# Two-stage set attention with a mixture of experts on one core: weights into score buffers, an eleventh x tile, and a new order of all steps

## The chip, the cores and the metric

One core of a Trainium2 chip runs the whole kernel. Its engines are PE (matrix products), DVE (vector), ACT (scalar), POOL (GpSimd) and SP, which issues the DMAs. The metric is the device time of one execution in microseconds (us), as a median of several runs. The language puts one instruction stream on each engine; waits between engines are semaphores.

## The reference

x has 4 batches (B) of N = 11456 rows of C = 128 floats; `inducing` has m = 32 rows. Everything is float32.

```python
def mab(q, kv):
    a = softmax(scale * (q @ kv.T))      # over kv, scale = 1/sqrt(C)
    return a @ kv
h = mab(I, x)        # per batch: 32 x 128 out of 11456 rows
t = mab(x, h)        # per batch: 11456 x 128
out = t.copy()       # then the mixture of experts on all B*N rows of t
do = t @ w_skip > 0
e = argmax(t[do] @ w_gate)                       # one of 8 experts
out[do] += prob(e) * (relu(t[do] @ w1[e]) @ w2[e])   # w1 128 x 1024, w2 1024 x 128
```

## The kernel before

A batch is cut into six groups of 1920 columns (the last 1856) of x transposed, [128, columns]; a group is one x tile of 960 KB, loaded by one DMA into one of ten buffers. Fourteen score buffers ("v", 128 x 960), three for transposed x ("xt"), three for exponentials ("e"), and eight PSUM banks ("banks") are shared the same way.

Per batch the program makes these steps. `load`: the x tiles, and for groups 2 and 3 of batches 1 to 3 also strips of x into v. `first` (lines 318 to 453): scores of x against the inducing rows on PE (L336), their maxima on DVE (L340, which also copies them into a v buffer), the common maximum (L345 on DVE, turned by PE at L348, L352 on DVE, spread by PE at L357), exponentials on ACT (L369), their transposition on DVE (L375), x transposed by PE (L379, copied out by ACT or DVE through the helper at L265/L267) or by DVE from strips (L388), and the sum over the tokens on PE (L395). `middle`: the division by the sums (DVE L472, "den"), the expert of the batch (L517 to L522), its weights read by SP (L651, L652) into an xt buffer, the expert applied to the 32 rows (`g_of` L571, `y_of` L624), the rows that turn a token's logits into relative ones (`lrq`, POOL L563). `second` for each unit of two groups (batch 3: two units of two, then two of one group, its half units): scores on PE (L679), transposition and maximum on DVE (L683, L685, one step `tokens`), the subtraction (L688, `less`, on POOL or DVE), exponentials on ACT, `fold` on POOL (L697), the sums (L701), division (L706, `norm`, POOL or DVE), transposition back (L713), gate logits on PE (L758), their transposition and largest (L762, L764, one step `relative_q`), the gate (L782, L783), `to_streams` on PE (L793), `scale2` (L801, a multiply of the whole tile by the gate, on POOL or DVE), and back again (L713). `emit` then makes the sums on PE (L845), copies them out by ACT or DVE, and SP stores them. `marking` and `judge` (L890 to L949) gather whether any token has another expert than its batch; if so a guarded path (`others`) corrects it, which is not entered with this data.

The order of all steps is a string, ORDER, decoded by `in_order` (L71): each entry names a step, one engine out of those that it allows, and the numbers of the buffers that it takes. Every engine runs its steps in that order, so an engine that waits holds back all that stands behind.

Of the kernel before, what the change touches and what calls it, by code (L numbers as in the profile page):

```python
# [9 lines left out]
F32 = mybir.dt.float32  # L10
# [60 lines left out]
def in_order(ops):  # L71
# [44 lines left out]
def kernel(  # L116
# [70 lines left out]
    sel = const.tile([P, 2 * M], F32, name="sel")
    nc.gpsimd.tensor_tensor(out=sel, in0=ident[:, 0:2 * M], in1=ident[:, 2 * M:], op=ALU.add)
    nc.gpsimd.tensor_tensor(out=sel[:, 0:M], in0=sel[:, 0:M], in1=sel[:, M:], op=ALU.add)
    nc.gpsimd.tensor_copy(out=rep.rearrange("p (q m) -> p q m", q=Q), in_=sel[:, 0:M].unsqueeze(1).broadcast_to([P, Q, M]))  # L190
# [8 lines left out]
    rows = const.tile([P, B, 2, M], F32, name="rows")  # L199
# [118 lines left out]
    def first(s, k):  # L318
# [135 lines left out]
    def middle(s):  # L454
# [119 lines left out]
        o, f = mm(g_of, "gr", s.o_hc, o_w)  # L574

# [51 lines left out]
        o, f = mm(y_of, "yp", o_g, o_w)  # L627
        o.free = [bg]
        L.add("POOL", lambda o: mend(o), o, free=[bw])

        def mend(o):
            nc.gpsimd.memset(xts[bw.idx][:, :, P:P + 1], 1.0)
# [15 lines left out]
    def load_w(e, t):  # L648
        t = t.rearrange("p i c -> p (i c)")
        w1s, w2s = t[:, 0:F], t[:, F:2 * F]  # L650
        nc.sync.dma_start(out=w1s, in_=w1[bass.ds(e, 1), :, :].rearrange("o c f -> c (o f)"))  # L651
        nc.sync.dma_start(out=w2s, in_=w2[bass.ds(e, 1)].rearrange("o p k c -> p (o k c)"))  # L652
# [482 lines left out]
```

## Time and profile before

| | before |
|---|---|
| median of 3 runs | 196.78 us (196.52 to 197.05) |
| profiled execution, its own time | 196.1 us |
| its span (first to last instruction) | 194.4 us |
| busy: PE, DVE, ACT, POOL | 172.8, 154.8, 111.2, 116.0 us |
| share of the span: PE, DVE, ACT, POOL | 89%, 80%, 57%, 60% |
| first DMA queue (x, strips, stores, weights) | 57.02 MB, 82.9% of the span |
| mean granted PE clock | 0.962 |

The slices of the page show PE busy at eight tenths or more in most of the span, DVE from about 50 us on, and both falling off at the end. The profiled execution is 0.68 us shorter than the median. The chain of work that ended last is 37% PE, 23% DVE and 22% DMA. No engine is the bound throughout, so below the span is cut where batch 0, 1, 2 and 3 reach L472, and where the last transposition back (L713) and the last sums (L845) end.

### The profile page before, as it was taken

How to read it: one execution, taken by the hardware profiler on the slowest of the kernel's cores; microseconds unless marked ns; L12 is line 12 of the kernel's file. 1: busy time of each engine (PE TensorE's matmuls, PEld its weight loads, DVE VectorE, ACT ScalarE, POOL GpSimd, SP SyncE). 2: the span in 40 equal slices, each digit the busy share in tenths (PEclk: the TensorE clock that was granted, in tenths of full speed). 3: DMA queues.
4: the chain of work that ended last, by engine and by line, in shares of the span. 5: the costliest groups of instructions: out<-in, count | busy, mean ns of one | idle time of the engine just before them, and what ended most of it. 6: DMA issues, size and time to landing. Idle time of an engine off the chain costs nothing.

```text
span 194.4 us, 5859 instructions
## 1 busy us (share of the span) xinstructions
PE 172.8 (89%) x2331; PEld 102.4 (53%) x2332; DVE 154.8 (80%) x288; ACT 111.2 (57%) x171; POOL 116.0 (60%) x225
## 2 busy tenths in 40 slices
PE   7998899997899999999999988999899698977910
PEld 7574684354687544366876523668545223423310
DVE  0455484798999989999999998999799988988320
ACT  3041680046981685887857564997356836597420
POOL 8200000276768669449986968687847987688510
PEclk9999999999999999999999999999999969999665
DMA  6999992789799799899997999489966995868690
GB/s 187 432 426 415 424 292 58 237 297 254 256 407 199 242 335 358 275 352 403 353 364 155 317 342 366 94 253 348 417 240 220 367 403 199 317 249 335 275 355 12
DMA packets 16881, 57.47 MB, mean 296 GB/s; under 512 B 2384, under 2 KB 7504, under 8 KB 16848
## 3 DMA queue, kind: packets, MB, share of 16 engines
q1 hardware_dynamic: 16560, 57.02, 82.9%
q8 instruction: 19, 0.31, 0.6%
q14 instruction: 14, 0.11, 0.2%
q10 hardware_dynamic: 288, 0.02, 0.1%
HBM read 33.58 MB, written 23.46 MB: 293 GB/s over the span
## 4 chain that ended last, share of the span: by engine, by line
PE 37%; DVE 23%; DMA 22%; ACT 5%; SPq 4%; issue 4%; POOL 2%; DVEq 0%; POOLq 0%; ACTq 0%
DMA x<-in_xT_dram 15%; PE banks L845 10%; PE banks L395 8%; PE banks L379 6%; DMA out_dram<-v 5%; DVE ts L685 3%; PE banks L336 3%; DVE e L683 3%; PE banks L679 3%; ACT v L265 3%; DMA v<-in_xT_dram 2%; DVE v L340 2%; PE banks L758 2%; DVE v L713 2%; SPq L279 2%
## 5 line engine op out<-in xcount | busy, mean ns | idle before, releaser
L265 ACT COPY v<-banks 128x960 f32<-128x960 f32 (+2 forms) x48 | 42.1, 935 | 9.3 <-PE banks L845 9.3
L688 POOL TENSOR_TENSOR e<-e,ts 128x960 f32<-128x960 f32 (+1 forms) x12 | 21.0, 1752 | 38.9 <-DVE ts L685 34.3
L265 ACT COPY xt<-banks 128x1024 f32<-128x1024 f32 (+1 forms) x31 | 28.9, 964 | 20.5 <-PE banks L379 20.4
L379 PE MATMUL banks<-ident,x 128*128 128x128 f32 x270 | 33.6, 276 | 0.0
L379 PEld LDWEIGHTS banks<-ident,x 128*128 128x128 f32 x270 | 29.4, 141 | 4.9 <-issue 1.7
L845 PE MATMUL banks<-v,hr 32*128 32x480 f32 (+1 forms) x192 | 28.5, 618 | 1.0 <-ACT v L265 1.0
L713 DVE STREAM_TRANSPOSE v<-e 128x960 f32<-128x960 f32 (+1 forms) x26 | 28.0, 1080 | 0.9 <-POOL e L801 0.2
L845 PE MATMUL banks<-v,yr 32*128 32x480 f32 (+1 forms) x192 | 26.6, 578 | 0.0
L395 PE MATMUL banks<-xt,v 128*32 128x129 f32 x720 | 25.0, 275 | 1.7 <-DVE v L375 1.1
L336 PE MATMUL banks<-x,iT_sb 128*32 128x480 f32 (+4 forms) x232 | 23.9, 503 | 1.6 <-DMA x<-in_xT_dram 1.6
L395 PEld LDWEIGHTS banks<-xt,v 128*32 128x32 f32 x720 | 20.8, 109 | 6.8 <-issue 2.1
L801 POOL TENSOR_TENSOR e<-e,gs 128x960 f32<-128x960 f32 x11 | 20.9, 1898 | 5.4 <-ACT gs L265 5.4
L679 PE MATMUL banks<-x,hc 128*32 128x480 f32 x192 | 22.5, 586 | 0.4 <-ACT hc L265 0.4
L706 POOL TENSOR_TENSOR e<-e,ts 128x960 f32<-128x960 f32 (+1 forms) x11 | 19.2, 1748 | 5.2 <-DVE ts L703 4.0
L340 DVE TENSOR_SCALAR_CACHE_REDUCE v<-banks 128x960 f32<-128x960 f32 (+1 forms) x13 | 13.9, 1067 | 9.1 <-PE banks L336 8.6
L691 ACT ACTIVATE e<-e 128x960 f32<-128x960 f32 (+1 forms) x13 | 12.3, 949 | 13.1 <-POOL e L688 11.0
L845 PEld LDWEIGHTS banks<-v,yr 32*128 32x128 f32 x192 | 11.5, 192 | 9.4 <-issue 8.6
L375 DVE STREAM_TRANSPOSE v<-v 128x960 f32<-128x960 f32 (+1 forms) x13 | 14.0, 1087 | 2.7 <-ACT v L369 2.6
L683 DVE STREAM_TRANSPOSE e<-banks 128x960 f32<-128x960 f32 (+1 forms) x13 | 14.1, 1086 | 1.3 <-PE banks L679 1.2
L845 PEld LDWEIGHTS banks<-v,hr 32*128 32x128 f32 x192 | 9.7, 189 | 9.4 <-issue 4.0
L685 DVE TENSOR_REDUCE ts<-e 128x30 f32<-128x960 f32 (+1 forms) x13 | 14.0, 1076 | 0.4
L369 ACT ACTIVATE v<-v,bias 128x960 f32<-128x960 f32 (+1 forms) x13 | 13.1, 1032 | 0.6 <-DVE bias L267 0.4
(147 smaller groups left out, 235.3 us busy)
## 6 DMA issues: line engine op xcount, KB each, us to landing
out_dram<-v SPq DMA_DIRECT2D x40, 480.0 KB, 4.5
x<-in_xT_dram SPq DMA_DIRECT2D x19, 960.0 KB, 9.6
v<-in_xT_dram SPq DMA_DIRECT2D x48, 120.0 KB, 6.7
xt<-in_w_dram SPq DMA_DIRECT2D x8, 512.0 KB, 5.4
x<-in_xT_dram SPq DMA_DIRECT2D x4, 928.0 KB, 8.1
out_dram<-v SPq DMA_DIRECT2D x6, 464.0 KB, 3.6
out_dram<-v SPq DMA_DIRECT2D x4, 232.0 KB, 2.7
x<-in_xT_dram SPq DMA_DIRECT2D x1, 512.0 KB, 4.0
```

What stands on the lines that cost most here:

```text
L265: nc.scalar.copy(out=out, in_=in_)
L336: nc.tensor.matmul(ps[q * M:(q + 1) * M, t * M:(t + v.shape[1]) * M].rearrange("m (t r) -> m t r", r=M), lhsT=iT_sb, rhs=v, start=True, st ...
L379: nc.tensor.transpose(out=pair(bp.idx)[:, j // Q, j % Q * P:(j % Q + 1) * P], in_=slot(s.xnow[g])[:, c:c + P], identity=ident)
L395: nc.tensor.matmul(ph[i * M:(i + 1) * M, 0:P + 1], lhsT=aT[:, j, t * M:(t + 1) * M], rhs=xts[bx.idx][:, t, :], start=begin and t < Q, stop ...
L679: nc.tensor.matmul(pair(bs.idx)[q * M:(q + 1) * M, j, 0:WB], lhsT=s.hc[:, 0:M], rhs=slot(bx)[:, G.s2[q]:G.s2[q] + WB], start=True, stop=True)
L683: nc.vector.transpose(out=by_j(ev(M)), in_=pair(bs.idx)[:, 0:n, 0:WB].rearrange("p j (t m) -> p j t m", m=M))
L685: nc.vector.tensor_reduce(out=mx[:, 0:nb], in_=ev(M), axis=AX.X, op=ALU.max)
L688: on(o).tensor_tensor(out=ev(M), in0=ev(M), in1=wide(st["mx"]), op=ALU.subtract)
L706: on(o).tensor_tensor(out=ev(M), in0=ev(M), in1=wide(st["i"]), op=ALU.mult)
L713: nc.vector.transpose(out=st[f"u{k}"][:, 0:W].rearrange("p (t m) -> p t m", m=M), in_=ev(M))
L801: on(o).tensor_tensor(out=ev(M), in0=ev(M), in1=wide(st["gm"]), op=ALU.mult)
L845: nc.tensor.matmul(pair(bp[q // 2].idx)[:, q % 2, 0:G.w1], lhsT=m[r, :], rhs=st[k][r, c:c + G.w1], start=(k == "u1"), stop=(k == "u2"))
```

## The change

The weights no longer share the xt buffers: `w1` and `w2` take a v buffer each, by two steps of SP, and POOL no longer restores the ones of an xt buffer (`mend`). With v tiles of 1024, xt tiles of 15 blocks instead of 16, and small tiles of the guarded path moved into the ends of xt tiles, room is made for an eleventh x tile.

```diff
-    BUFS = {"x": 10, "v": 14, "xt": 3, "e": 3, "lt": 3, "gsel": 1, "fd": 2}
+    BUFS = {"x": 11, "v": 14, "xt": 3, "e": 3, "lt": 3, "gsel": 1, "fd": 2}
...
-    shapes = {"x": [GC], "v": [2, WB], "fd": [WIDE * HALF], "lt": [2 * NQ * E]}
+    shapes = {"x": [GC], "v": [VW], "fd": [WIDE * HALF], "lt": [2 * NQ * E]}
...
-    xts = [const.tile([P, 2 * F // P, P + 1], F32, name=f"xt{i}") for i in range(BUFS["xt"])]
+    xts = [const.tile([P, -(-GC // P), P + 1], F32, name=f"xt{i}") for i in range(BUFS["xt"])]
...
-            st["w1"], st["w2"] = load_w(e1, xts[bw.idx])
-
-        bw = Buf("xt")
-        o_w = L.add("SP", weights, o_c, take=[bw])
+            st["e1"], st["w1"] = e1, slots["v"][b1.idx]
+            load_1(e1, st["w1"])
+
+        def weights2(o):
+            st["w2"] = slots["v"][b2.idx]
+            load_2(st["e1"], st["w2"])
+
+        b1, b2 = Buf("v"), Buf("v")
+        o_w = L.add("SP", weights, o_c, take=[b1])
+        o_w2 = L.add("SP", weights2, o_c, behind=[o_w], take=[b2])
```

`tokens` and `relative_q` are cut in two steps each (the same instructions, which ORDER may now put apart). The maxima of the gate logits are no longer kept to the end: `claim_q` subtracts on the spot (one more small POOL instruction a unit), and the four POOL pairs of `theirs` (L919, L920) are gone.

```diff
+        def highest(o):
             mx = st["mx"] = tsmall[be.idx][0]
             nc.vector.tensor_reduce(out=mx[:, 0:nb], in_=ev(M), axis=AX.X, op=ALU.max)
...
+        def largest_q(o):
+            mx = st["gx"] = gsmall[blt.idx][1]
             nc.vector.tensor_reduce(out=mx[:, 0:nq], in_=qv()[:, :, 0:E - 1], axis=AX.X, op=ALU.max)
...
+            nc.gpsimd.tensor_tensor(out=p, in0=p, in1=t, op=ALU.subtract)
...
-        o_n = L.add("POOL", theirs, *s.o_claim)
```

The guarded path loads its weights in eight pieces and x in four, and one more memset stands inside it. ORDER is new from end to end, of which a line shows nothing:

```diff
-    "000006100H11001090J1207200I20K20810092D0O1320Q110R302080A20B140C20U100D150E20F30G2C0M30P30N2B0i1110k120l20307040605050V1"
+    "0000010A061007200H1100I302090J120K308100O1120P30Q120R3092D0A20B100U130308040705060C20D120E30i1010F30G2C0k113005310432033"
```

By it, three of the five copies of transposed x on DVE go to ACT; the one `less` on DVE (a half unit, L688) goes to POOL; of the `scale2` multiplies DVE has two full ones and a half one where it had two half ones. PE's work and the bytes moved are the same in all.

On PE, around the common maximum of batch 1 (a row is line, operation, output<-inputs, shape and count; x tiles and buffers carry the program's numbers). Before:

```order
L336 MATMUL banks<-x_150,iT_sb 32x480 x4
L336 MATMUL banks<-x_149,iT_sb 32x448 x4
L336 MATMUL banks<-x_149,iT_sb 32x32 x4
L379 MATMUL banks<-ident,x_145 128x128 x8
L571 MATMUL banks<-xt_194,hc_517 32x256 x4
L348 MATMUL banks<-ident,low_1_648 1x128
L357 MATMUL banks<-ones,rows 32x1 x4
L584 MATMUL banks<-ident,g_0_646 128x128 x2
L379 MATMUL banks<-ident,x_145 128x128 x7
L758 MATMUL banks<-v_159,lrq_200 32x256 x4
L395 MATMUL banks<-xt_193,v_158 32x129 x15
```

The same place after the change (L348, L360, L369 and L391 there are L336, L348, L357 and L379 of before):

```order
L348 MATMUL banks<-x_143,iT_sb 32x448 x4
L348 MATMUL banks<-x_143,iT_sb 32x32 x4
L703 MATMUL banks<-x_134,hc_514 32x480 x4
L703 MATMUL banks<-x_144,hc_514 32x480 x4
L391 MATMUL banks<-ident,x_139 128x128 x7
L360 MATMUL banks<-ident,low_1_594 1x128
L348 MATMUL banks<-x_142,iT_sb 32x480 x4
L369 MATMUL banks<-ones,rows 32x1 x4
L391 MATMUL banks<-ident,x_138 128x128 x15
L348 MATMUL banks<-x_141,iT_sb 32x480 x4
L784 MATMUL banks<-v_145,lrq_196 32x256 x4
```

Scores of batch 2 (x_142, x_141) now stand between the turn and the spread and behind them, a whole tile's transposition instead of half a one, and the sum over the tokens comes later.

On DVE, in the last stretch, where batch 3's half units begin. Before:

```order
L611 TENSOR_REDUCE gmax<-banks 128x8
L683 STREAM_TRANSPOSE e_133<-banks 128x15x32
L685 TENSOR_REDUCE ts_0_171<-e_133 128x15
L688 TENSOR_TENSOR e_133<-e_133,ts_0_171 128x15x32
L701 TENSOR_REDUCE sums<-e_134 128x15
L703 RECIPROCAL ts_1_174<-sums 128x15
L713 STREAM_TRANSPOSE v_160<-e_135 128x960
```

After (L707, L711 and L830 are L683, L685 and L801 of before):

```order
L707 STREAM_TRANSPOSE e_127<-banks 128x15x32
L788 STREAM_TRANSPOSE lt_161<-banks 128x256
L711 TENSOR_REDUCE ts_2_168<-e_127 128x15
L830 TENSOR_TENSOR e_125<-e_125,gs_2_184 128x30x32
L792 TENSOR_REDUCE gs_0_171<-lt_161 128x32
L739 STREAM_TRANSPOSE v_153<-e_125 128x960
...
L830 TENSOR_TENSOR e_126<-e_126,gs_0_174 128x30x32
L792 TENSOR_REDUCE gs_2_181<-lt_163 128x16
L739 STREAM_TRANSPOSE v_150<-e_126 128x960
```

The half subtraction left DVE, and two whole multiplies by the gate came to it.

On PE, at the end. Before:

```order
L845 MATMUL banks<-v_165,hr_1915 128x480 x4
L845 MATMUL banks<-v_160,yr_2181 128x480 x4
L845 MATMUL banks<-v_153,hr_1915 128x464 x4
L845 MATMUL banks<-v_163,yr_2181 128x464 x4
L893 MATMUL banks<-ident,lo_2296 1x128
```

After (L876 and L924 are L845 and L893 of before):

```order
L876 MATMUL banks<-v_154,hr_1849 128x464 x4
L876 MATMUL banks<-v_156,yr_2187 128x464 x4
L876 MATMUL banks<-v_152,hr_1849 128x480 x4
L876 MATMUL banks<-v_145,yr_2187 128x480 x4
L924 MATMUL banks<-ident,lo_2360 1x128
```

The last group and the one before it changed places.

## Rows read from the trace of the kernel before

**Rows 1.** Busy time by stretch: length, then each engine's busy us, clock, DMA share, GB/s

```profile
core 0: us, PE busy (x) PEld busy (x) DVE busy (x) ACT busy (x) POOL busy (x), PEclk, DMA share, GB/s
0.00:31.84 31.84, 28.95 (x388) 21.94 (x393) 14.43 (x28) 11.64 (x16) 5.54 (x46) 1.00 0.91 341
31.84:62.40 30.56, 28.14 (x422) 17.20 (x422) 27.98 (x49) 15.18 (x23) 17.82 (x26) 1.00 0.82 256
62.40:100.85 38.45, 38.45 (x556) 22.76 (x555) 36.85 (x63) 28.13 (x41) 28.43 (x42) 1.00 0.95 338
100.85:138.81 37.96, 35.95 (x548) 21.95 (x550) 35.16 (x69) 25.61 (x38) 29.40 (x40) 1.00 0.87 277
138.81:181.10 42.29, 37.02 (x405) 16.45 (x405) 38.33 (x73) 27.34 (x47) 32.55 (x63) 0.94 0.78 301
181.10:184.30 3.20, 3.20 (x25) 1.29 (x17) 0.29 (x1) 1.82 (x2) 1.39 (x7) 0.71 0.51 202
184.30:194.40 10.10, 1.09 (x5) 0.80 (x4) 1.71 (x9) 1.53 (x4) 0.83 (x4) 0.60 0.50 191
```

**Rows 2.** DVE's instructions by line and shape: count, busy us, mean ns, idle before

```profile
L713 DVE STREAM_TRANSPOSE v<-e 128x960 f32<-128x960 f32 x22 | 25.4, 1155 | 0.8 <-POOL e L801 0.2 <-issue 0.2
L340 DVE TENSOR_SCALAR_CACHE_REDUCE v<-banks 128x960 f32<-128x960 f32 x11 | 12.6, 1142 | 3.0 <-PE banks L336 2.5 <-DMA out_dram<-v 0.5
L701 DVE TENSOR_REDUCE sums<-fd 128x30 f32<-128x510 f32 x9 | 5.9, 653 | 0.0
L762 DVE STREAM_TRANSPOSE lt<-banks 128x256 f32<-128x256 f32 x11 | 4.6, 422 | 1.1 <-PE banks L758 1.1
L764 DVE TENSOR_REDUCE gxs<-lt 128x32 f32<-128x224 f32 x11 | 4.2, 386 | 0.4
L701 DVE TENSOR_REDUCE sums<-e 128x30 f32<-128x990 f32 x2 | 2.3, 1160 | 0.0
L801 DVE TENSOR_TENSOR e<-e,gs 128x480 f32<-128x480 f32 x2 | 1.6, 780 | 0.1
L706 DVE TENSOR_TENSOR e<-e,ts 128x480 f32<-128x480 f32 x1 | 0.7, 659 | 0.1
```

**Rows 3.** PE's scores of two tiles, in order of time (start, length)

```profile
72.49 1.82 PE L336 MATMUL banks<-x,iT_sb 128*32 128x480 f32 x16
```

**Rows 4.** What PE waited for, 31.84 to 138.81 us: total, times, longest

```profile
PE banks L395 <- DVE v L375: 0.9, 1, 0.9
PE banks L336 <- DMA x<-in_xT_dram: 0.8, 1, 0.8
PE banks L348 <- DVE low L345: 0.7, 1, 0.7
```

**Rows 5.** What PE waited for, 138.81 to 181.10 us

```profile
PE banks L793 <- POOL lt L786: 1.5, 2, 1.3
PE banks L758 <- POOL lrq L563: 1.3, 1, 1.3
```

**Rows 6.** DVE in order of time, last stretch: start, length, instruction, idle before

```profile
151.02 1.83 DVE L706 TENSOR_TENSOR e<-e,ts 128x960 f32<-128x960 f32 x1
...
157.14 0.45 DVE L762 STREAM_TRANSPOSE lt<-banks 128x256 f32<-128x256 f32 x1 [0.52 <-PE banks L758]
...
167.28 2.30 DVE L688 TENSOR_TENSOR e<-e,ts 128x480 f32<-128x480 f32 x1
```

**Rows 7.** POOL in order of time, the same stretch

```profile
150.03 1.81 POOL L688 TENSOR_TENSOR e<-e,ts 128x960 f32<-128x960 f32 x1 [0.51 <-DVE ts L685]
151.80 2.73 POOL L801 TENSOR_TENSOR e<-e,gs 128x960 f32<-128x960 f32 x1
...
167.25 1.81 POOL L801 TENSOR_TENSOR e<-e,gs 128x960 f32<-128x960 f32 x1 [0.71 <-ACT gs L265]
```

**Rows 8.** PE in order of time, the end

```profile
180.49 1.84 PE L845 MATMUL banks<-v,yr 32*128 32x480 f32 x8
182.09 1.40 PE L845 MATMUL banks<-v,hr 32*128 32x464 f32 x8
183.31 0.96 PE L845 MATMUL banks<-v,yr 32*128 32x464 f32 x8
```

More of the change, by code (lines that the diff above doesn't have):

```diff
@@ L23 @@
 WIDE = 2 * (WB // M)
+VW = 1024
 NQ = 32
+WPIECES = 8
+XPIECES = 4
 BANKS = 8
@@ L178 @@
         nc.gpsimd.memset(codes[:, e:e + 1], float(E - e))
-    sums = const.tile([P, B, NU, NQ], F32, name="sums")
+    NB = 3 * NQ
+    sums = const.tile([P, B, NB], F32, name="sums")
     nc.gpsimd.memset(sums, float(M))
-    posm = const.tile([P, B, NU, NQ], F32, name="posm")
+    posm = const.tile([P, B, NB], F32, name="posm")
     nc.gpsimd.memset(posm, 0.0)
-    gxs = const.tile([P, B, NU, NQ], F32, name="gxs")
-    nc.gpsimd.memset(gxs, 0.0)
     rep = const.tile([P, P], F32, name="rep")
[L187 to L190, printed above, removed]
     zero = const.tile([P, 1], F32, name="zero")
@@ L197 @@
     marks = const.tile([P, 2, B], F32, name="marks")
-    rows = const.tile([P, B, 2, M], F32, name="rows")
+    rows = const.tile([P, B + 1, M], F32, name="rows")
     nc.gpsimd.memset(rows, 0.0)
@@ L202 @@
     nc.gpsimd.memset(lows, 0.0)
-    gexps = const.tile([P, 2, MAXB // 2, E + 1], F32, name="gexps")
-    nc.gpsimd.memset(gexps, 1e-9)
     qexps = [const.tile([P, NQ, E], F32, name=f"qexp{i}") for i in range(BUFS["lt"])]
@@ L350, in least @@
         def least(o):
-            st["mn"] = rows[:, b, k, :]
+            st["mn"] = rows[:, B if k else b, :]
             nc.vector.tensor_reduce(out=st["mn"][0:1], in_=bank(f1.idx)[0:1, 0:P].rearrange("o (q m) -> o m q", m=M), axis=AX.X,
@@ L574, in middle @@
         o, f = mm(g_of, "gr", s.o_hc, o_w)
+        o.free = [b1]
         def g_rows(o):
@@ L625, in y_of @@
                                  start=(k < Q), stop=(k >= KF - Q))
[L627 to L632, printed above, removed]
+        o, f = mm(y_of, "yp", o_g, o_w2)
+        o.free = [bg, b2]
         def parts(o):
@@ L641, in rows @@
         def rows(o):
-            s.yr = perb.tile([P, P], F32, tag="yr", bufs=3, name=f"yr_{b}")
+            s.yr = perb.tile([P, P], F32, tag="yr", bufs=2, name=f"yr_{b}")
             copy(o, s.yr, st["y"][:, 0:P])
@@ L646, in middle, with load_w, load_1, load_2 @@
         return L
[L648 to L652, printed above, removed]
-        return w1s, w2s
+    def load_w(e, w1s, w2s, n):
+        load_1(e, w1s, n)
+        load_2(e, w2s, n)
+        return w1s, w2s
+    def load_1(e, t, n=1):
+        for i in range(n):
+            c = slice(i * F // n, (i + 1) * F // n)
+            nc.sync.dma_start(out=t[:, c], in_=w1[bass.ds(e, 1), :, c].rearrange("o c f -> c (o f)"))
+    def load_2(e, t, n=1):
+        for i in range(n):
+            c = slice(i * F // n, (i + 1) * F // n)
+            k = slice(i * KF // n, (i + 1) * KF // n)
+            nc.sync.dma_start(out=t[:, c], in_=w2[bass.ds(e, 1), :, k].rearrange("o p k c -> p (o k c)"))
     def second(s, u, gs, bxs, main):
@@ L699, in total @@
         def total(o):
-            r = sums[:, b, u, :] if keep else wk.tile([P, NQ], F32, tag="r2", name=f"r2_{b}_{gs[0].col0}")
+            r = sums[:, b, u * (NQ // 2):] if keep else cols[4]
             nc.vector.tensor_reduce(out=r[:, 0:nb], in_=ev(M + 1) if st["whole"] else halved(), axis=AX.X, op=ALU.add)
@@ L804, in second @@
         o = L.add("DVE", tokens, o, free=[bs])
+        o = L.add("DVE", highest, o)
         o = L.add("POOL DVE", less, o)
@@ L813, in second @@
             o = L.add("PE", logits_q, o, s.o_lrq, take=[bl, blt])
-            o_m = L.add("DVE", relative_q, o, free=[bl])
+            o = L.add("DVE", relative_q, o, free=[bl])
+            o_m = L.add("DVE", largest_q, o)
             o_x = L.add("ACT", gexp_q, o_m)
@@ L889, in lowest @@
             lo = st["lo"] = perb.tile([P, 1], F32, tag="lo", name=f"lo_{b}")
-            nc.vector.tensor_reduce(out=lo, in_=sums[:, b].rearrange("p g t -> p (g t)"), axis=AX.X, op=ALU.min)
+            nc.vector.tensor_reduce(out=lo, in_=sums[:, b], axis=AX.X, op=ALU.min)
         def turn(o):
@@ L931, in marking @@
         o = L.add("POOL", unsure, o, *s.o_sizes)
-        s.o_marks = [L.add("DVE", any_unsure, o), L.add("DVE", strangers, o_n)]
+        s.o_marks = [L.add("DVE", any_unsure, o), L.add("DVE", strangers, *s.o_claim)]
         return L
@@ L1020, in other_group @@
         x = slot(bx)
-        nc.sync.dma_start(out=x[:, 0:G.cols], in_=xT[bass.ds(s.at, 1), :, bass.ds(col0, G.cols)].rearrange("o c n -> c (o n)"))
+        step = G.cols // XPIECES
+        for i in range(XPIECES):
+            nc.sync.dma_start(out=x[:, i * step:(i + 1) * step],
+                              in_=xT[bass.ds(s.at, 1), :, bass.ds(col0 + i * step, step)].rearrange("o c n -> c (o n)"))
         def gates(st, lv, gv, two):
-            tmp = lambda k, bufs=2: wk.tile([P, NQ], F32, tag=f"t{k}", name=f"t{k}_{b}_{col0}")
-            c = wk.tile([P, 2, MAXB // 2, E], F32, tag="tc", bufs=1, name=f"tc_{b}_{col0}")
+            c = cells
             cv = c[:, :, 0:nh, :]
@@ L1082, in all_steps @@
             ops += middle(s)
-            for u, ul in enumerate(SECOND[b]):
+            at = 0
+            for ul in SECOND[b]:
+                u, at = at, at + len(ul)
                 st, L = second(s, u, [s.groups[g] for g in ul], [s.xbuf[g] for g in ul], None)
```

81 lines of the change are left out of this document (45 added, 36 removed).

## The prediction

> **What bounds the kernel now.** I read the busy time cut into stretches first, since the averages of the page mix unlike things. Up to batch 0's "den" (31.84 us) the DMA share is 0.91 and DVE is busy for 14.43 us only: loading sets the pace [rows 1]. From there to the last transposition back at 181.10, PE and DVE are both nearly full: DVE works 27.98, 36.85, 35.16 and 38.33 us in stretches of 30.56, 38.45, 37.96 and 42.29 us, so it idles 2.58, 1.60, 2.80 and 3.96, or 10.94 us of 149.26; PE fills the third stretch entirely [rows 1]. So neither a transfer nor one engine is the limit; the time is DVE's work plus what DVE idles, except in the third stretch, where PE is as long. Behind that comes a tail: 3.20 us of PE's last sums at a granted clock of 0.71, and 10.10 us of gathering the marks and leaving [rows 1].
>
> The other views say where the two wait for each other. PE waits once for x after the first stretch (0.8 us), and 0.7 to 0.9 us around a common maximum, for its minimum and then for the scores turned by DVE [rows 4]. In the last stretch it waits 1.5 us for the gates of the half units and 1.3 for `lrq` from POOL [rows 5].
>
> **The change part by part.** I counted DVE's rows in the order before and after between the four dens and priced the differences by shape [rows 2]; terms under 0.4 us are given as one net figure.
>
> First stretch (to 31.84): DVE loses three copies of transposed x to ACT. DVE has 17 us of room there and the loads the same bytes, so I take 0. If ACT became late with them, hsum of batch 0 would be; ACT is busy for only 11.64 us [rows 1], so that is covered. An eleventh tile means that twelve loads are queued at the start; the queue serves them in order and the first ones come no sooner. Loads of weights now stand on SP's queue behind the x tiles and strips of the next batch; they wait for two v buffers instead of an xt. With the one later x wait of 0.8 us [rows 4] I also put the eleventh buffer itself at 0, bounded by that 0.8 above and by a late weight load below, for which the nearest row is POOL's 1.3 us wait [rows 5].
>
> Second stretch (30.56): DVE gains one maxima of a batch 2 tile (+1.14) and loses a folded sum (−0.65), a largest (−0.39) and small ones (net −0.84 with the former's reciprocal): 27.98 − 0.74 = 27.2. The holes of 0.7 and 0.4 that PE had around the turn now hold 0.91 us of scores (half of 1.82 [rows 3]), as the order shows. DVE idle kept at 2.6: **29.8**.
>
> Third stretch (38.45): a back (−1.16), two maxima (−2.28), two logit transpositions (−0.84), one largest (−0.39) and one sum over the unfolded tile (−1.16) go out; two folded sums (+1.30) and small ones (+0.9) come in: 36.85 − 3.6 = 33.3. PE loses three tiles' scores (3 × 0.91 = 2.7) and smaller things, 0.7 net: 38.45 − 3.4 = 35.1. PE bounds; with 0.4 of waiting **35.5**.
>
> Fourth stretch (37.96): maxima +1.14, a logit transposition +0.42, small terms −2.3: 35.16 − 0.7 = 34.5. PE loses one tile of last sums and gains two tiles of scores, 35.95 − 0.6 = 35.3; it idled 2.0 here, 0.8 of which was the wait for x [rows 4], which the eleventh buffer should remove: 35.3 + 1.2 = **36.5**.
>
> So batch 3's den comes at 31.84 + 29.8 + 35.5 + 36.5 = 133.6, 5.2 us earlier.
>
> Fifth stretch (42.29): what was taken out above has to be done here, and more multiplies. Out go the half subtraction (−2.30 [rows 6]), one half gate multiply (−0.78) and a minimum (−0.26). In come two whole gate multiplies, a back (+1.16), two largest (+0.77), a logit transposition (+0.42), and 1.6 of gate sums, reciprocal and copies. A whole gate multiply on DVE is in no row. The nearest is the whole `norm` multiply of the same shape at 1.83 us [rows 6]; from below it is bounded by twice 0.66 less its overhead, about 1.0, from above by a start right behind a POOL multiply, about 1.0 after POOL's 1.81 us, or 2.8 [rows 2, 7]. I take 1.83, two of them 3.66. Sum: 38.33 + 4.3 = 42.6.
>
> That 1.83 us is itself a contended price. POOL's multiply at 150.03 ended at 151.84, and DVE's, begun at 151.02, ended at 152.85, 1.0 later; POOL's next, begun at 151.80, took 2.73 instead of 1.81. At 167.28 a half multiply on DVE took 2.30 beside a POOL multiply, where alone it took 0.66 [rows 2, 6, 7]. The two engines' multiplies delay one another. So I add 0.7 of POOL's 0.92 to DVE's idle, as one such victim on the way. Idle before was 3.96; the wait for `lrq` (0.52 on DVE before L762 [rows 6], and as much again around it) should go, since PE now has about 9 us of other rows between den's logits and that product: 3.0. Together 42.6 + 3.0 + 0.7 = 46.3, **last back at 179.9**.
>
> The Trainium skill, "SBUF — State Buffer", section "Who interferes with whom", says that a DVE instruction with two SBUF inputs and a GpSimd instruction that reads SBUF exclude each other for the whole instruction, the later one blocking. The rows above agree; by the rule taken to its end, each of the moved multiplies would cost 2.8 or delay POOL as long, and the sum would be 2 to 3 us higher.
>
> Tail: before, PE's last sums ended 3.2 us after the last back because it still had both groups' rows to do; now only one group's second half (1.84 at low clock [rows 8]) depends on the last back: 1.9. The exit stays at 10.1 (`judge` is unchanged; the POOL pair that is gone, L919 and L920, ended before). A low clock is kept in this price; at full clock it would be 0.9 less.
>
> End: 179.9 + 1.9 + 10.1 = 191.9 against 194.4, a gain of 2.5 us. The profiled execution took 196.1, so 193.6; it lies 0.7 below the median of 196.78, and so I predict **194.3**. Other small ones: `claim_q` gains one POOL instruction a unit and loses four pairs, POOL is busy for 116 of 194 us; tokens cut in two, the same work. Guarded pieces are not run. All 0.
>
> **The rivals.**
>
> *The last stretch takes more than the earlier ones give* (slower). The mechanism is the multiplies on DVE, 4.3 us of added work in the stretch that sets the end, paid only if batch 3's den comes earlier. If PE and DVE stay coupled so that it still comes at 138.8: 138.81 + 42.6 + 3.96 + 1.9 + 10.1 = 197.4, as a time 199.1, as a median 199.8. It decides at a den of 136.1: then 136.1 + 46.3 + 1.9 is the 184.3 of before. For it speaks that the third and fourth stretches have PE and DVE both over 92% busy, and nothing guarantees that each idles less when it has less to do. Against it: 4.3 us of DVE and 3.4 us of PE work do leave those stretches. 0.21.
>
> *The multiplies block each other in full*: two at 2.8 instead of 1.83, +1.9, and POOL's successors +0.3: 196.5. That is the rule of the page made a mechanism; one start in two in the rows is that bad. 0.07.
>
> *The change only moves the idle time*: the DVE work is 0.7 us less (−0.74 − 3.6 − 0.7 + 4.3), the 10.94 of idle stays, and the blocking of 0.7 eats it; tail as before. That includes that the eleventh buffer does nothing, since the loads waited for no one but once. 196.8. 0.08.
>
> *Multiplies fall free of POOL and the clock stays up at the end*: −1.7 (two at 1.0), −0.7, −0.9: 191.0. 0.14.
>
> **How the numbers follow.** Forecast 0.50, with 192.8 to 196.1 by itself. A measurement of this kernel tells about 0.3%, 0.6 us, from no change. Faster (under 196.2): 0.50 + 0.14 = 0.64; within: 0.07 + 0.08 = 0.15; slower (over 197.4): 0.21. The range from 191.5 to 198.3 leaves out about half of the best case and the larger half of the slower one, 0.18.
>
> **What would show it.** Batch 3's den at about 133.6 and the stretches at 29.8, 35.5, 36.5 and 46.3; no wait of PE for `lrq` over 0.5; the two whole gate multiplies on DVE at 1.0 to 2.8, with POOL's neighbours at 2.7 where they met; PE's last sums within 2 us of the last back. A den at 136 or later, or DVE idle of 5 us and more in the last stretch, would make it wrong, and a wait for the weights or the x tiles before 133 would name the reason.

## The result and the profile after

The changed kernel takes 187.18 us (187.09 to 187.80, 4 runs) against 196.92 us for the kernel before, run beside it (196.52 to 197.15, 4 runs): a ratio of 0.9615, 95% interval 0.956 to 0.967. That is 9.7 us less, where 2.5 was forecast; the time lies 4.3 us under the lower end of the range. On another chip it measured 0.9607 (0.956 to 0.9655). On the chips of the experiments single executions of one program lie several us apart, the longer ones mostly at the lower mean clock (the kernel before: 192.49 us at 0.989, 199.45 at 0.954), and a ratio takes only those within 1.5% of their own kernel's fastest. So the experiments below are read by stretches of a profile first, and by times only where these are clear.

Busy time by stretch, profile after, cut at the same events as [rows 1] (the columns are those of rows 1):

```profile
0.00:31.68 31.68, 29.10 (x388) 21.96 (x393) 11.15 (x23) 14.40 (x20) 4.65 (x44) 1.00 0.96 363
31.68:59.94 28.26, 27.88 (x431) 17.59 (x432) 26.51 (x47) 15.17 (x23) 16.24 (x24) 1.00 0.92 289
59.94:94.57 34.63, 34.63 (x502) 21.76 (x504) 32.84 (x59) 25.93 (x39) 26.94 (x35) 1.00 0.83 292
94.57:132.81 38.24, 35.05 (x533) 21.19 (x525) 34.32 (x65) 25.79 (x39) 29.34 (x46) 1.00 0.84 273
132.81:177.07 44.26, 39.64 (x471) 18.10 (x473) 39.30 (x83) 29.64 (x51) 35.22 (x72) 1.00 0.88 329
177.07:178.89 1.82, 1.82 (x21) 0.91 (x13) 1.48 (x7) 1.00 (x2) 0.35 (x2) 1.00 1.00 393
178.89:186.10 7.21, 0.98 (x6) 0.64 (x5) 1.20 (x8) 1.82 (x2) 0.82 (x4) 0.81 0.71 268
```

The first column after the colon pair is the length, and against [rows 1] it tells where 8.3 us of span went, in us:

| stretch | before | forecast | after |
|---|---|---|---|
| to batch 0's den | 31.84 | 31.84 | 31.68 |
| to batch 1's | 30.56 | 29.8 | 28.26 |
| to batch 2's | 38.45 | 35.5 | 34.63 |
| to batch 3's | 37.96 | 36.5 | 38.24 |
| to the last back | 42.29 | 46.3 | 44.26 |
| to PE's last sums | 3.20 | 1.9 | 1.82 |
| to the end | 10.10 | 10.1 | 7.21 |

Batch 3's den comes at 132.81 (133.6 forecast), so the shape was right: the second and third stretch give, the fifth takes. The sizes were not: the fourth stretch came 1.7 us above its forecast, the fifth 2.0 below, and the exit 2.9 below. PE keeps its full clock (1.00) down to 178.89 us, where before it fell to 0.94 and 0.71 [rows 1].

What PE waits for in the profile after, 59.94 to 178.9 us (total, times, longest), and then, in order of time, DVE's whole multiplies of the fifth stretch (L732 a division, L830 the two by the gate) and POOL's rows beside them:

```profile
PE banks L822 <- POOL lt L815: 1.2, 3, 0.7
PE banks L348 <- ACT v L277: 1.2, 1, 1.2
PE banks L589 <- DMA v<-in_w_dram: 0.9, 1, 0.9
...
PE banks L369 <- DVE rows L364: 0.9, 1, 0.9
```

```profile
150.15 1.16 DVE L732 TENSOR_TENSOR e<-e,ts 128x960 f32<-128x960 f32 x1
...
159.63 1.15 DVE L830 TENSOR_TENSOR e<-e,gs 128x960 f32<-128x960 f32 x1
...
166.69 1.84 DVE L830 TENSOR_TENSOR e<-e,gs 128x960 f32<-128x960 f32 x1
```

```profile
159.79 1.84 POOL L714 TENSOR_TENSOR e<-e,ts 128x480 f32<-128x480 f32 x1 [1.11 <-DVE ts L711]
...
163.22 0.20 POOL L634 TENSOR_SCALAR gabs<-pos 128x8 f32<-128x8 f32 x1
...
163.66 1.00 POOL L732 TENSOR_TENSOR e<-e,ts 128x480 f32<-128x480 f32 x1
...
166.51 1.00 POOL L714 TENSOR_TENSOR e<-e,ts 128x480 f32<-128x480 f32 x1 [1.04 <-DVE ts L711]
167.47 1.11 POOL L634 TENSOR_SCALAR gabs<-pos 128x8 f32<-128x8 f32 x1
```

The wait for `lrq` [rows 5] is gone, as forecast; a new one of 0.9 us for weights is there (of the kind I had bounded by 1.3), and one of 1.2 us for ACT's copy out of the banks (L277). The multiplies are read further down, where the prediction is compared with them.

### The profile page after: what moved, and what is told of

Same layout as the page of the kernel before. It is cut to its first block, busy times and chain, and to the rows that moved or that the text cites. A ratio compares the mean times of both kernels' runs of the same rounds, so it can differ in the third digit from the quotient of the medians.

```text
span 186.1 us, 5857 instructions
## 1 busy us (share of the span) xinstructions
PE 169.1 (91%) x2331; PEld 102.1 (55%) x2332; DVE 146.8 (79%) x285; ACT 113.7 (61%) x175; POOL 113.6 (61%) x224
## 4 chain that ended last, share of the span: by engine, by line
PE 55%; DMA 18%; DVE 11%; issue 4%; SPq 4%; ACT 3%; POOL 3%; DVEq 0%; ACTq 0%
DMA x<-in_xT_dram 13%; PE banks L876 12%; PE banks L391 12%; PE banks L407 9%; PE banks L348 8%; PE banks L703 6%; DMA out_dram<-v 3%; DVE v L739 2%; DMA v<-in_w_dram 2%; SPq L304 2%; ACT v L277 2%; PE banks L784 2%; SPq L291 1%; PE banks L589 1%; DVE lt L788 1%
## 5 line engine op out<-in xcount | busy, mean ns | idle before, releaser
L277 ACT COPY v<-banks 128x960 f32<-128x960 f32 (+2 forms) x47 | 42.4, 939 | 15.6 <-PE banks L876 10.6
L714 POOL TENSOR_TENSOR e<-e,ts 128x960 f32<-128x960 f32 (+1 forms) x13 | 22.8, 1756 | 36.9 <-DVE ts L711 36.9
L277 ACT COPY xt<-banks 128x896 f32<-128x896 f32 (+1 forms) x34 | 31.3, 957 | 12.7 <-PE banks L391 12.7
L391 PE MATMUL banks<-ident,x 128*128 128x128 f32 x270 | 33.3, 275 | 0.0
L391 PEld LDWEIGHTS banks<-ident,x 128*128 128x128 f32 x270 | 29.5, 141 | 3.6 <-issue 1.2
L876 PE MATMUL banks<-v,hr 32*128 32x480 f32 (+1 forms) x192 | 27.6, 597 | 1.3 <-ACT v L277 0.9
L876 PE MATMUL banks<-v,yr 32*128 32x480 f32 (+1 forms) x192 | 25.8, 564 | 0.6 <-DVE v L739 0.6
L348 PE MATMUL banks<-x,iT_sb 128*32 128x480 f32 (+4 forms) x232 | 24.2, 509 | 1.8 <-ACT v L277 1.2
L407 PE MATMUL banks<-xt,v 128*32 128x129 f32 x720 | 23.2, 274 | 0.0
L703 PE MATMUL banks<-x,hc 128*32 128x480 f32 x192 | 22.0, 571 | 0.4 <-ACT hc L277 0.4
L732 POOL TENSOR_TENSOR e<-e,ts 128x960 f32<-128x960 f32 (+1 forms) x11 | 19.2, 1744 | 3.6 <-DVE ts L729 3.1
L830 POOL TENSOR_TENSOR e<-e,gs 128x960 f32<-128x960 f32 (+1 forms) x10 | 17.3, 1733 | 5.0 <-ACT gs L277 3.4
L717 ACT ACTIVATE e<-e 128x960 f32<-128x960 f32 (+1 forms) x13 | 12.4, 957 | 11.4 <-POOL e L714 11.4
L723 POOL TENSOR_TENSOR fd<-e 128x510 f32<-128x510 f32 (+1 forms) x11 | 12.9, 1169 | 9.8 <-ACT e L717 8.7
L876 PEld LDWEIGHTS banks<-v,yr 32*128 32x128 f32 x192 | 11.6, 185 | 9.4 <-issue 6.3
L707 DVE STREAM_TRANSPOSE e<-banks 128x960 f32<-128x960 f32 (+1 forms) x13 | 14.1, 1084 | 1.8 <-PE banks L703 1.7
L876 PEld LDWEIGHTS banks<-v,hr 32*128 32x128 f32 x192 | 9.8, 183 | 9.2 <-ACT v L277 3.2
L711 DVE TENSOR_REDUCE ts<-e 128x30 f32<-128x960 f32 (+1 forms) x13 | 13.8, 1060 | 0.1
```

Of the source, the lines that this page charges most:

```text
L277: nc.scalar.copy(out=out, in_=in_)
L348: nc.tensor.matmul(ps[q * M:(q + 1) * M, t * M:(t + v.shape[1]) * M].rearrange("m (t r) -> m t r", r=M), lhsT=iT_sb, rhs=v, start=True, st ...
L391: nc.tensor.transpose(out=pair(bp.idx)[:, j // Q, j % Q * P:(j % Q + 1) * P], in_=slot(s.xnow[g])[:, c:c + P], identity=ident)
L407: nc.tensor.matmul(ph[i * M:(i + 1) * M, 0:P + 1], lhsT=aT[:, j, t * M:(t + 1) * M], rhs=xts[bx.idx][:, t, :], start=begin and t < Q, stop ...
L703: nc.tensor.matmul(pair(bs.idx)[q * M:(q + 1) * M, j, 0:WB], lhsT=s.hc[:, 0:M], rhs=slot(bx)[:, G.s2[q]:G.s2[q] + WB], start=True, stop=True)
L714: on(o).tensor_tensor(out=ev(M), in0=ev(M), in1=wide(st["mx"]), op=ALU.subtract)
```

## Experiments

Each is the changed kernel with one part undone, or the kernel before with one part done. In the forecast three parts stood at nothing: the guarded path's pieces, the eleventh tile, and the steps cut in two.

**Pieces of the guarded path**, taken out of the changed kernel, and put into the kernel before alone:

```diff
-WPIECES = 8
-XPIECES = 4
+WPIECES = 1
+XPIECES = 1
```

```diff
-        w1s, w2s = load_w(e, xts[2])
+        w1s, w2s = load_w(e, xts[2], 8)
...
-        nc.sync.dma_start(out=x[:, 0:G.cols], in_=xT[bass.ds(s.at, 1), :, bass.ds(col0, G.cols)].rearrange("o c n -> c (o n)"))
+        step = G.cols // 4
+        for i in range(4):
+            nc.sync.dma_start(out=x[:, i * step:(i + 1) * step],
+                              in_=xT[bass.ds(s.at, 1), :, bass.ds(col0 + i * step, step)].rearrange("o c n -> c (o n)"))
```

> The changed kernel, with the weights and x of the guarded path (not entered) loaded in one piece each instead of eight and four. Theory A: the exit, 10.1 us from PE's last sums to the end before and 7.2 after, got shorter because of the guarded path's code; then this run's exit is about 2.5 us longer than 7.2 and the time about 189.7. Theory B: the pieces matter nothing when they are not executed; then 187.2 within 0.5 and an exit of 7.2.

> The kernel before, with the guarded path's weights in eight pieces and its x in four, nothing else. Theory A: the exit falls from 10.1 us by about 2.4 and the time to about 194.4. Theory B: 196.8 within 0.5, exit of 10.1.

The exit can be read from two rows of each profile: its span, and the last instruction of DVE (`anyi`, the judge's verdict). Before:

```profile
span 194.4 us, 5859 instructions
...
188.60 0.16 DVE L949 TENSOR_REDUCE anyi<-two 128x1 int32<-128x8 f32 x1
```

After:

```profile
span 186.1 us, 5857 instructions
...
182.17 0.16 DVE L974 TENSOR_REDUCE anyi<-two 128x1 int32<-128x8 f32 x1
```

The changed kernel with one piece each:

```profile
span 190.0 us, 5857 instructions
...
184.56 0.16 DVE L974 TENSOR_REDUCE anyi<-two 128x1 int32<-128x8 f32 x1
```

The kernel before with pieces:

```profile
span 193.2 us, 5859 instructions
...
189.94 0.16 DVE L954 TENSOR_REDUCE anyi<-two 128x1 int32<-128x8 f32 x1
```

From the end of `anyi` to the end of the span it is 5.6 us before, 3.8 after, 5.3 after with one piece, and 3.1 before with pieces. (The profile with one piece is of the longest of its four executions, 191.81 us where the others took 188.64 to 189.99, so only its exit is read here.) The other profiles agree: 5.7 us with lrq early, the only other one without pieces, and 3.5 to 3.8 in the nine others. So theory A holds for the exit, in both directions: code that is jumped over and never run costs or saves 1.5 to 2.5 us at the end of the program. In the trace SP stands still between two of its last semaphore instructions for 2.4 us before (from 190.97) and 1.9 with one piece (from 187.72), and nowhere so long with pieces. The times do not show it: before with pieces gives a ratio of 0.9994 (0.993 to 1.005), which leaves out the 1.2% of theory A, and in its profile batch 3's den came 1.3 us later (140.07 for 138.81), which takes half of the gain back. Why the longer skipped code gives the shorter exit, and whether it is its length, its DMAs or its place, is in no row of these views, and stays open.

**lrq early before, late after.** On POOL, in the kernel before, five rows (L558 to L563) move up past three:

```diff
 L548 COPY lr_210<-pl_1966 128x2
+L558 TENSOR_SCALAR r_3_2013<-codes,code_1972 128x7
...
+L563 TENSOR_TENSOR lrq_212<-r_3_2013,cmask 128x32
 L697 TENSOR_TENSOR fd_166<-e_133 128x510
 L688 TENSOR_TENSOR e_135<-e_135,ts_2_175 128x30x32
 L801 TENSOR_TENSOR e_134<-e_134,gs_0_181 128x30x32
```

In the changed kernel the same five (L576 to L581) move down, past two whole subtractions, some small steps, a fold and the gate multiply at 152.25 us.

> The kernel before, with batch 3's step on POOL that makes lrq moved in front of the gate multiply (2.73 us) that it stood behind; PE waited 1.30 us for it at 155.9, and its granted clock fell to half from there to about 159.2. Theory C (the hole in PE's work costs more than its length, since the clock falls behind it): the clock stays at 1.0 through 150 to 165 us and the time falls by 2 to 3 us, to about 194.3. Theory D (the wait is covered by DVE's work or replaced by another wait): the time falls by at most 0.5, whatever the clock does.

> The changed kernel, with batch 3's step on POOL that makes lrq moved behind the gate multiply at 152.25 us, so that PE waits about 2 us for it at 153.3. Theory C: the clock falls to half for some 3 us behind the wait, and the time rises by 2.5 to 4 us, to about 190.2. Theory D: the rest of the last stretch takes up the wait; at most 1 us, to 188.2.

The kernel before with lrq early, where the wait had been, its last stretch and its tail:

```profile
155.00:160.00 5.00, 4.15 (x35) 1.76 (x34) 4.90 (x10) 2.79 (x6) 3.61 (x7) 1.00 1.02 406
...
139.24:180.10 40.86, 36.00 (x405) 16.88 (x405) 38.04 (x73) 27.43 (x47) 32.48 (x63) 0.98 0.81 312
180.10:183.30 3.20, 3.20 (x25) 1.24 (x18) 0.28 (x1) 1.71 (x2) 1.39 (x7) 0.74 0.47 186
```

The changed kernel with lrq late, around the wait and in the whole stretch, and the wait:

```profile
153.00:156.00 3.00, 0.88 (x12) 0.12 (x8) 2.05 (x3) 2.41 (x3) 2.76 (x7) 1.00 1.02 405
156.00:160.00 4.00, 4.00 (x46) 1.53 (x48) 3.30 (x8) 2.00 (x4) 3.61 (x8) 1.00 0.81 321
...
133.10:178.60 45.50, 38.98 (x471) 18.40 (x473) 39.52 (x83) 29.42 (x51) 35.70 (x74) 1.00 0.85 317
```

```profile
PE banks L784 <- POOL lrq L581: 2.1, 1, 2.1
```

In the kernel before the stretch shrank by 1.4 us (42.29 to 40.86), about the 1.3 us of the hole, and the mean clock over it was 0.98 instead of 0.94 [rows 1]. Half of theory C came true there: the clock stayed at 1.00 where it had fallen to 0.50 behind the wait. The other half did not, since the gain is the length of the wait and no more. In the changed kernel a hole of 2.1 us was followed by PE at full clock and cost 1.2 to 1.5 us (45.50, where two profiles of the changed kernel have 44.26 and 43.98). So theory C falls as I put it: a hole cost about its own length or less, and the clock did not answer to this one. The timed comparisons do not show the gain (1.0016, 0.995 to 1.009, against before) and are too scattered for the loss (0.973, 0.956 to 0.990, for the late one).

**Both edits in the kernel before** (pieces and lrq early):

> The kernel before with the guarded path in pieces and lrq's step early, together. In their profiles the first made the exit 2.5 us shorter (3.1 for 5.6, from the judge's load to the end) and the second the last stretch 1.4 us. If the two are independent: exit 3.1, last stretch 40.9, span about 190.5, and a time about 4 us below the kernel before on the same chip. Rival: the gain of the second is taken up, and only 2.5 us show.

```profile
140.40:181.25 40.85, 36.02 (x413) 16.84 (x413) 38.03 (x73) 27.51 (x48) 32.45 (x63) 1.00 0.79 304
181.25:182.70 1.45, 1.45 (x17) 0.49 (x9) 0.29 (x1) 1.45 (x2) 1.12 (x7) 1.00 0.97 389
182.70:190.70 8.00, 1.09 (x5) 0.80 (x4) 1.71 (x9) 1.68 (x5) 1.03 (x5) 0.70 0.65 250
```

192.49 us, ratio 0.9835 (0.977 to 0.991): 3.2 us less (1.8 to 4.6), with no other buffer and no other change of order. The interval holds the rival's 2.5 too; it is the stretches that speak for the sum, with 40.85 us for the fifth and 3.5 from `anyi` to the end. That the span (190.7) is near the sum of the two (190.5) is in part chance: batch 3's den came 1.6 us later (140.40 for 138.81), and PE's tail took 1.45 us at full clock instead of 3.20 at 0.71 [rows 1], with 17 instructions left in it instead of 25. With lrq early alone it had still taken 3.20 at 0.74, so which step kept the clock up is not shown.

**Ten x tiles** in the changed kernel; three loads and one set of strips come later and the x tiles are numbered anew, everything else stands in its order:

```diff
-    BUFS = {"x": 11, "v": 14, "xt": 3, "e": 3, "lt": 3, "gsel": 1, "fd": 2}
+    BUFS = {"x": 10, "v": 14, "xt": 3, "e": 3, "lt": 3, "gsel": 1, "fd": 2}
```

> The changed kernel with ten x tiles instead of eleven: three x loads (and one set of strips) are issued later, behind the step that frees a tile, everything else in the same order. Theory E (the eleventh tile is what lets the scores of the next batch stand early): PE waits for x and the time rises by 1 us or more, to 188.2 or above. Rival, as in the prediction: the eleventh tile is worth 0, since PE waited for x only once in the kernel before; 187.2 within 0.5.

199.90 us, ratio 1.021 (1.013 to 1.029) to the kernel before. Its second and third stretches, what PE waited for in the second, and SP's loads there:

```profile
32.13:68.00 35.87, 29.56 (x431) 17.91 (x432) 26.85 (x48) 15.28 (x23) 16.30 (x24) 0.90 0.91 274
68.00:105.60 37.60, 34.75 (x502) 21.73 (x504) 32.89 (x59) 25.97 (x39) 26.89 (x35) 1.00 0.76 268
```

```profile
PE banks L348 <- DMA x<-in_xT_dram: 5.5, 1, 5.5
...
```

```profile
35.10 5.75 SPq L304 DMA_DIRECT2D v<-in_xT_dram  x8
41.06 1.39 SPq L291 DMA_DIRECT2D x<-in_xT_dram  x3
```

In the changed kernel the three loads go out together at 34.28 us, here at 41.06:

```profile
34.28 3.55 SPq L291 DMA_DIRECT2D x<-in_xT_dram  x3
```

The stretch grew from 28.26 to 35.87 us, far more than the 1 us of theory E. The eleventh tile is no small part of this order: without it, the last x of batch 1 is issued 6.8 us later, behind strips that were held back with the load ahead of it, and PE stands 5.5 us. Behind that wait the clock fell, too: PE was busy for 29.56 us at a mean clock of 0.90 with the 431 matmuls that took 27.88 at 1.00, which is 1.7 us on top of the wait. Other places for the held strips were not tried, so this is the price of ten tiles in this order, not of ten tiles.

**Maxima back behind their transpositions**: all, then those of the scores, then those of the logits. One of the places, on DVE:

```diff
 L707 STREAM_TRANSPOSE e_126<-banks 128x30x32
-L364 TENSOR_REDUCE rows<-banks 1x32
 L711 TENSOR_REDUCE ts_1_166<-e_126 128x30
+L364 TENSOR_REDUCE rows<-banks 1x32
```

> The changed kernel with each maximum of scores again right behind its transposition on DVE, and each largest gate logit right behind the transposition of the logits (19 of the 26 pairs had DVE steps between them). Theory: placing them apart lets DVE free banks earlier, so undoing it costs 0.5 to 1.5 us, to about 188.2. Rival: it is the same work on an engine with 5 us of idle time in the last stretch; 187.2 within 0.5.

> The changed kernel with only the maxima of scores put back behind their transpositions (10 of 13 had DVE steps between them). With all pairs joined the stretch from batch 0's den to batch 1's grew by 1.7 us and the whole by about 4. Theory H: it is the whole-tile maximum (1.15 us) that stands in the way of short DVE steps PE waits for, so this part holds most of it: 190 or above, and the stretch to batch 1's den near 30.0. Rival: the logits' maxima hold it; then 187.2 to 188 here.

> The changed kernel with only the largest gate logits put back behind the transpositions of the logits (9 of 13 had DVE steps between them; 0.39 us each). Theory H: little, 187.2 to 188.0. Rival: they hold most of the 4 us, 190 or above.

DVE around batch 1's common maximum in the changed kernel:

```profile
43.69 1.17 DVE L707 STREAM_TRANSPOSE e<-banks 128x960 f32<-128x960 f32 x1
44.78 0.24 DVE L364 TENSOR_REDUCE rows<-banks 1x32 f32<-1x128 f32 x1
44.95 1.13 DVE L711 TENSOR_REDUCE ts<-e 128x30 f32<-128x960 f32 x1
```

and with all pairs joined, with what PE waited for there and the stretch:

```profile
44.20 1.17 DVE L707 STREAM_TRANSPOSE e<-banks 128x960 f32<-128x960 f32 x1
45.41 1.15 DVE L711 TENSOR_REDUCE ts<-e 128x30 f32<-128x960 f32 x1
46.48 0.27 DVE L364 TENSOR_REDUCE rows<-banks 1x32 f32<-1x128 f32 x1
```

```profile
PE banks L369 <- DVE rows L364: 1.2, 1, 1.2
```

```profile
32.05:62.04 29.99, 28.40 (x434) 17.94 (x434) 27.51 (x49) 15.29 (x23) 16.65 (x24) 1.00 0.92 273
```

All joined: 191.41 us, ratio 0.978 (0.970 to 0.985), where the changed kernel has 0.9607: about 3.4 us, more than I expected. The rows show one of the ways: 0.27 us of work that PE waits for stands behind 1.15 us that it does not wait for, and the stretch is 1.3 to 1.7 us longer than in two profiles of the changed kernel (28.66, 28.26).

They show a second way. Where a DVE row reads what the row before it wrote, it begins 0.03 us behind that row's end (above, 45.41 behind 44.20 + 1.17); where it does not, and nothing else holds it, it begins 0.08 us ahead of it (44.78, ahead of 43.69 + 1.17): these are the medians over all neighbours less than 0.15 us apart, in the profiles of before, after and all joined alike. Of neighbours that depend on one another so there are 92 before, 69 after and 89 with all joined; 20 times 0.11 is 2.2 us, and DVE's busy time grew by 1.8 (146.8 to 148.6).

With the scores alone the second stretch is 29.6, with the logits alone 28.9. The ratios are 0.965 (0.957 to 0.973) and 0.9665 (0.960 to 0.973); both overlap the changed kernel's (0.956 to 0.9655), and hardly reach the 190 us of theory H and of the other run's rival. The scores matter more in that stretch, but that either part holds most of the whole is not shown, so theory H is not confirmed.

**A hole beside the spread**, scores of a batch 2 tile behind it on PE:

```diff
 L360 MATMUL banks<-ident,low_1_594 1x128
+L369 MATMUL banks<-ones,rows 32x1 x4
 L348 MATMUL banks<-x_142,iT_sb 32x480 x4
-L369 MATMUL banks<-ones,rows 32x1 x4
```

> The changed kernel with the scores of one batch 2 tile on PE moved from between the turn and the spread of batch 1's common maximum to behind the spread. PE then waits for the spread's row again. Theory G: PE is the bound from 32 us on, so the time rises by the hole, 0.6 to 1.0 us, to about 188.0. Rival: the hole is caught up at the next wait; 187.2 within 0.3.

PE's wait, and the stretch:

```profile
PE banks L369 <- DVE rows L364: 1.0, 1, 1.0
```

```profile
31.98:61.10 29.12, 27.80 (x430) 17.52 (x430) 26.87 (x47) 15.24 (x23) 16.23 (x24) 1.00 0.92 273
```

0.5 to 0.9 us more than the two profiles of the changed kernel have here (28.66, 28.26), where PE has no such wait, and nothing of it comes back in the next stretch (34.70 where they have 34.67 and 34.63): theory G, though those two profiles themselves lie 0.4 apart. The time is 189.17 us, with an interval (0.957 to 0.977) that overlaps the changed kernel's.

**The two whole gate multiplies on POOL**, one of the two places on DVE:

```diff
 L711 TENSOR_REDUCE ts_2_168<-e_127 128x15
-L830 TENSOR_TENSOR e_125<-e_125,gs_2_184 128x30x32
 L792 TENSOR_REDUCE gs_0_171<-lt_161 128x32
```

> The changed kernel with the two whole gate multiplies of batch 3 on POOL (1.8 us each) instead of DVE (1.15 and 1.84 us measured). Theory F: POOL, busy 35.2 of 44.3 us in that stretch, becomes late; the time rises by 1 to 2.5 us, to about 189. Rival, the prediction's price for them on DVE (they and POOL's multiplies delay one another): DVE gains 3 us and the time falls by 0.5 to 1.5, to about 186.2.

What DVE waited for in the last stretch:

```profile
DVE v L739 <- POOL e L830: 5.3, 2, 2.7
...
```

190.44 us, ratio 0.968 (0.961 to 0.975). No gain, so the rival falls; how much worse it is the scatter does not tell (the changed kernel's interval, 0.956 to 0.9655, overlaps). The waits show theory F's way: DVE stood 5.3 us for the two multiplies, and the last stretch took 46.22 us instead of 44.26 and 43.98 (the profile is of the longest of its five executions, but PE's clock was 1.00 in this stretch).

**The changed kernel again**, as a reference on one of those chips:

> The changed kernel unaltered, as the reference on this chip for the runs beside it: 187.2 within 0.6, stretches between batches' dens as in its first profile (31.7, 28.3, 34.6, 38.2, 44.3 us), and an exit of 3.7 us from the judge's load to the end.

187.77 us (187.50 to 188.97, 6 runs), stretches 31.95, 28.66, 34.67, 37.94, 43.98. Two profiles of the same kernel agree within 0.4 us a stretch, which is what the readings above can bear.

## Why the prediction was wrong

The direction and the shape were right and most terms were mis-sized; together they make 7.1 us (194.3 forecast, 187.18 measured). The changes in the exit and by the cut steps stood at nothing, and DVE's work was priced too high: in the four stretches between the first den and the last transposition back it was busy for 132.97 us instead of 138.32, 5.4 less where my terms took off 0.7. It also idled more, 12.4 us instead of 10.9, where the sum had 10.5, so the errors cancelled in part.

*"The exit stays at 10.1"* and *"Guarded pieces are not run. All 0."* It took 7.21: 1.9 us less behind the judge, which the profiles with and without pieces show, and 1.0 less in front of it, in the marks, which no run separates. That is 2.9 us, the largest step that failed.

*Fifth stretch, 46.3.* It took 44.26. I added 4.3 us of DVE work; DVE's busy time grew by 0.97 (38.33 to 39.30). The whole multiplies cost 1.15 and 1.84 against 1.83 each: I took for both the price of one that POOL holds up, and only one of them met that. The division that gave the price [rows 6] took 1.16 itself after the change. And the length of a row is more than it adds, since consecutive DVE instructions overlap (44.78 + 0.24 ends after 44.95 above): in this stretch the lengths add up to 41.1 us before and 43.6 after, 2.5 more, and the overlap grew from 2.8 to 4.3. Against that DVE idled 4.96 us, where the sum had 3.7.

*Tail, 1.9.* It took 1.82, by luck. I had one half of one group's rows at the low clock; PE did both halves of it at the full one:

```profile
177.00 1.09 PE L876 MATMUL banks<-v,hr 32*128 32x480 f32 x8
177.80 1.09 PE L876 MATMUL banks<-v,yr 32*128 32x480 f32 x8
```

*Second and third stretch, 29.8 and 35.5.* They took 28.26 and 34.63. The steps cut in two stood at 0 ("the same work"), and joining them again costs 1.3 to 1.7 us in the second stretch, 0.5 in the third (35.13) and some 3.4 in all: the same work, but in front of PE's wait or behind it, and end to end or overlapped. The scores that fill PE's hole were named but brought nothing in the sum, where DVE's idle time was kept at 2.6; it was 1.75, and emptying the hole again costs 0.5 to 0.9.

*"I also put the eleventh buffer itself at 0, bounded by that 0.8."* The bound was read from an order made for ten tiles, where nothing could ask for an eleventh. The new order asks for it: with ten it takes about 12 us more, by the ratios. It is not the tile that gains 12, but the order as it stands needs it.

*Fourth stretch, 36.5*, took 38.24: the wait of 0.8 for x did go (0.2 left), but PE waits 1.2 for ACT, 0.9 for the row of the spread and 0.9 for weights in its place: 3.2 us of idle time where the sum had 1.2. The wait for weights (it ended at 128.2) is the sign that the prediction had named.

*The offset.* I set the profile 0.7 below the median, as before; after, the profiled execution (187.8) lay 0.6 above. That is 1.3 us of the 7.1, and chance.

*The rivals.* "The last stretch takes more" had the right mechanism and the wrong sign of the balance: the den came at 132.8, well before the 136.1 from which it would have decided. Two multiplies at 2.8 did not come: of the two, which both met POOL, one began 0.16 us ahead and kept its 1.15, POOL's half then taking 1.84 for 1.00; the other came 0.18 behind and took 1.84, ending 1.0 after POOL, and POOL's next small row, begun at 167.47, took 1.11 where a row of the same line and shape took 0.20 at 163.22. That agrees with the Trainium skill, "SBUF — State Buffer", "Who interferes with whom": the first to issue goes, the other blocks. Each meeting cost the later row a little less than what was left of the earlier one (0.84 of 0.99, 0.69 of 0.82, 0.91 of 1.06 us), and in the second both engines paid in turn. The nearest rival, "Multiplies fall free of POOL and the clock stays up at the end" (191.0), had the clock right and one of the multiplies, and was still 3.8 us over. "The change only moves the idle time" was right that idle time stays, and wrong that the work does.

What no run tells: what the weights in score buffers are worth by themselves (to undo it needs xt tiles of 16 blocks and other places for the transposed x), and what the clock is worth in the gain as a whole (one price stands above, 1.7 us behind a wait of 5.5). That the new order keeps the clock up is seen in the profiles; by which step, the runs with lrq did not show.

## What to carry to other kernels

A resource or a cut of steps that the old order does not wait for may be what the new order is built on: price it with the new order's demands, not from the old waits. Ask of each short step that another engine waits for what long step stands ahead of it on its own engine; the cut of a step in two adds no work, lets it pass, and here also let neighbours on one engine overlap. And measure the exit by itself, from the last useful instruction to the end of the span: it was 5.6 of 194 us here, and code that never ran changed it.

## What the runs showed of the hardware

A DVE instruction that reads what the one before it wrote began 0.03 us behind its end; one that did not, and that nothing else held, began 0.08 us ahead of it (medians). Code that is never entered changed the program's exit by 1.5 to 2.5 us (3.1 to 3.8 us with the guarded loads in pieces, 5.3 to 5.7 without). A hole of 2.1 us in PE's work passed without a fall of the clock in the changed kernel, while in the kernel before PE ran at half clock (0.50, the lower of its two levels, 1.2 GHz) behind the wait of 1.30 us that ended at 155.9, as this stretch of it shows:

```profile
156.00:158.00 2.00, 2.00 (x14) 0.61 (x18) 1.45 (x4) 0.96 (x2) 1.96 (x2) 0.50 1.01 401
```

Executions of the kernel before on one chip had mean clocks from 0.954 to 0.989, and the two at the ends took 199.45 and 192.49 us.
